# FFN weight scales from sums of squares taken ahead, a new order of the down phase, and weight work inside the units alone

## The chip, the cores and the metric

The kernel runs on one core of one Trainium2 chip. Its time is device time in microseconds: 2755.78 us is the median of three runs of the kernel before (2755.2 to 2758.46). The core has a matrix engine (PE; its weight loads are listed apart as PEld), three engines for elementwise work (DVE, ACT, POOL), and a queue engine (SP) that issues most DMAs. Each engine takes its instructions in the order in which the program gives them; they wait for each other through semaphores.

## The reference, cut to what matters

One transformer block in float32: a sequence S of 2048 rows, width D = 576, 32 heads of 18, and a gated FFN of width 4608.

```python
def _A_ref(x, wqkv, wo):
    qkv = (x @ wqkv).reshape(B, S, 3, H, Dh).transpose(2, 0, 3, 1, 4)
    q, k, v = qkv[0], qkv[1], qkv[2]
    p = _softmax(jnp.einsum("bhqd,bhkd->bhqk", q, k) * Dh ** -0.5, axis=-1)
    return jnp.einsum("bhqk,bhkd->bhqd", p, v).transpose(0, 2, 1, 3).reshape(B, S, D) @ wo

def _B_ref(x, w_gate, w_up, w_down):
    g = jnp.einsum("bsd,df->bsf", x, w_gate)
    u = jnp.einsum("bsd,df->bsf", x, w_up)
    return jnp.einsum("bsf,fd->bsd", _gelu(g) * u, w_down)

h = x + _A_ref(_layernorm(x, axis=-1), A_wqkv, A_wo)
h2 = h + _B_ref(_layernorm(h, axis=-1), B_w_gate, B_w_up, B_w_down)
```

`w_gate` and `w_up` are 576 x 4608, `w_down` is 4608 x 576. The change lies in the last line (`_B_ref`), and in a piece of the attention phase in which weights for it are read ahead.

## The kernel before, in words

Float32 operands are split into two float16 parts, high and low, after multiplication by a power of two; a product is high·high + high·low + low·high, accumulated in PSUM. The power of two comes from an exponent of the weight block. `exponents` finds it: DVE takes the largest magnitude of each partition (L129), PE turns the 128 maxima into a row (L138, a transpose), DVE takes the maximum of that (L142) and shifts out its exponent. `pow2` makes the scale (`p_s_m`, `p_s_dn`).

After attention comes the FFN. The hidden width is cut into 18 chunks of 256 columns, and a loop over `sc` takes two chunks, c and c+1, at a time. The rows are in two halves, p = 0 and p = 1. One pass of the loop, called a round below, runs for the chunks c and c+1 on p = 1 and the next two on p = 0:

```text
unit(c,1)  unit(c+1,1)  down7(1)  unit(c+2,0)  unit(c+3,0)  down7(0)
```

`unit` forms gate and up with Strassen's seven products (Winograd's form): 14 products of 7 matmuls each (L1175), alternately for gate (banks g) and up (banks u), called product 0 to 13 here. ACT copies banks out, since a bank is accumulated on later: product 10 adds to the gate bank that product 8 wrote, so it waits for ACT's copy of it (L1226); product 11 waits for L1230. GELU (L1180) is on ACT, sums and the gating (L1183) on DVE, the hidden value's high part (L1191) on ACT and its low part (L1194) on POOL. The last two products leave a tail on DVE (L1258, L1183, L1266, L1267). After `yield` number k a step of other work can be taken from an iterator `side`; `beside` does that.

`down7` does the down projection of two chunks with seven products as well (HA11 ... HS4), each for two row tiles k. It accumulates in three pairs of banks, X, B and Z (L1286), and DVE adds the bank to the output rows in `nat` (L1291; L1296 adds one bank to both halves). The eight row tiles then leave to DRAM (`nat_d`, L1301) and the other half's tiles are fetched (L1320).

The side work is the weights of the chunks to come. A matrix (gate or up) of a chunk is loaded by eight DMAs on SP (`load_matrix`, L977 and L979) into four of the eight parts of the buffer W8. There is one W8, so the next load waits for the last reads of this one. `split_matrix` then takes the exponent, forms four sums on POOL (L993, S1 to S4), and cuts them to float16: ACT writes three high parts (L1013: parts 4 to 6, which need the DMAs alone, then S1 and S2, then S3 and S4) and DVE the low parts (L1027, L1029). After the first low part the load of the next matrix is issued. `split_down7` scales the down weights (L1136), forms sums on POOL (L1138 to L1145) and cuts seven parts (L1132 on ACT, L1133 on DVE).

The order on PE, ACT, DVE, POOL and, after attention, SP is that of the code, written by hand. In the kernel before, a round's side work starts in unit(c,1) with the exponent of the first matrix, cuts that matrix in unit(c+1,1), and runs on through down7(1), unit(c+2,0) and unit(c+3,0). The exponents of the first two chunks are taken in the attention phase: while the first row maxima of the attention are formed, a loop of 30 steps runs 'sums', a chain that ends in `raw_norms`, on raw weights that POOL's DMAs bring to WK (`raw_loads`).

## Time and profile before

| | |
|---|---|
| median of 3 runs | 2755.78 us |
| the profiled execution | 2758.85 us, span 2757.0 us |
| busy in the span | PE 94%, DVE 84%, ACT 63%, POOL 38% |
| attention, with what stands ahead of it | until about 1,400 us |
| FFN rounds | about 151 us each |
| granted TensorE clock, mean | 0.977 |

The span runs from the first to the last instruction; the profiled execution's 2758.85 us has 1.85 us around it, and lies 3.07 us above the median. PE's busy share says little here: a matmul's recorded time contains its passage through the array, so matmuls overlap in the records. What a stage loses is read from the starts of the products, and from the idle time before an instruction, which the timeline gives in square brackets with what ended it.

### The profile page before, as it was taken

To read this page: it belongs to the slowest core of one execution; us is meant where nothing else is said; L and a number is where in the kernel's file an instruction comes from. 1 tells how busy PE (TensorE), PEld (TensorE's weight loads), DVE (VectorE), ACT (ScalarE), POOL (GpSimd) and SP (SyncE) were. 2 spreads that over 40 slices of the span, in tenths; PEclk is the share of its full clock that TensorE was granted. 3 is DMA by queue.
4 is the path that set the end of the run, shared out by engine and by line. 5 is a ranking of instruction groups with operands and counts; after the bars stand their busy time and mean duration, and the time that the engine had idled before them with its cause. 6 is when DMAs were issued, how large, how long until landed. Compare 5 with 4: busy or idle time off the path is not lost.

```text
span 2757.0 us, 54241 instructions
## 1 busy us (share of the span) xinstructions
PE 2594.8 (94%) x20381; PEld 1174.7 (43%) x20381; DVE 2321.2 (84%) x4230; ACT 1740.0 (63%) x3260; POOL 1034.9 (38%) x1274
## 2 busy tenths in 40 slices
PE   8999999999999999999999988898989898988989
PEld 4533333333333333333355545454445454544545
DVE  7479999999999999998676778788787878787885
ACT  6229999999999999997744334343343433343432
POOL 4202532323232323235853344444443334434432
PEclk9999999999999999999999999999999999999999
DMA  8521010101010101011344223222222223232212
GB/s 221 139 90 30 19 44 16 44 16 42 16 45 16 44 17 42 18 30 36 70 99 88 73 80 101 97 70 76 91 90 90 99 88 107 80 111 86 79 62 82
DMA packets 204761, 189.06 MB, mean 69 GB/s; under 512 B 92504, under 2 KB 151404, under 8 KB 204498
## 3 DMA queue, kind: packets, MB, share of 16 engines
q1 hardware_dynamic: 195758, 169.27, 20.6%
q0 software_dynamic: 8608, 16.33, 2.4%
q8 instruction: 159, 2.61, 0.4%
q14 instruction: 104, 0.85, 0.1%
q10 hardware_dynamic: 132, 0.01, 0.0%
HBM read 115.44 MB, written 50.40 MB: 60 GB/s over the span
## 4 chain that ended last, share of the span: by engine, by line
PE 70%; DVE 16%; issue 5%; ACT 3%; DMA 2%; POOL 2%; SPq 1%; DVEq 0%; ACTq 0%; POOLq 0%
PE bank L673 18%; PE more L1175 8%; PE bank L1175 7%; PE quad L615 7%; PE bank L615 6%; PE more L1286 4%; PE bank L1286 4%; PE quad L300 4%; PE quad L665 4%; PE bank L300 4%; PE bank L665 3%; DVE mx L625 3%; PE more L300 1%; DMA A<-in_B_w_up_dram 1%; DVE W L1029 1%
## 5 line engine op out<-in xcount | busy, mean ns | idle before, releaser
L667 ACT ACTIVATE WK<-quad 128x512 f32<-128x512 f32 x1170 | 656.3, 621 | 26.0 <-PE quad L665 23.6
L673 PE MATMUL bank<-WK,V 128*32 128x256 f32 x8192 | 607.7, 389 | 2.6 <-DVE nat L688 0.6
L625 DVE TENSOR_REDUCE mx<-quad 128x1 f32<-128x512 f32 x836 | 554.0, 685 | 9.0 <-PE quad L665 1.5
L667 ACT ACTIVATE WK<-bank 128x512 f32<-128x512 f32 x878 | 504.9, 622 | 12.0 <-PE bank L665 10.2
L625 DVE TENSOR_REDUCE mx<-bank 128x1 f32<-128x512 f32 x716 | 477.3, 685 | 35.5 <-PE bank L615 26.8
L1175 PEld LDWEIGHTS <-W 128*128 128x128 f16 x2394 | 242.6, 101 | 341.4 <-issue 85.5
L673 PEld LDWEIGHTS bank<-WK,V 128*32 128x32 f32 x8192 | 190.4, 109 | 268.5 <-issue 201.9
L698 POOL TENSOR_TENSOR rp<-rc,minus_one 128x4 f32<-128x4 f32 x112 | 111.2, 1012 | 380.1 <-DMA rc<-nat 377.9
L1175 PE MATMUL bank<-X,W 128*128 128x512 f16 x792 | 225.3, 382 | 0.0
L993 POOL TENSOR_TENSOR A<-A 128x384 f32<-128x384 f32 x136 | 142.7, 1065 | 193.3 <-DVE V L1208 99.3
L1175 PE MATMUL bank<-V,W 128*128 128x512 f16 x720 | 212.3, 395 | 0.5 <-ACT WK L1217 0.5
L615 PE MATMUL quad<-W 54*128 54x512 f16 x514 | 191.3, 383 | 0.0
L1286 PEld LDWEIGHTS <-WK 128*128 128x128 f16 x1472 | 147.3, 100 | 97.1 <-issue 54.2
L1286 PE MATMUL more<-nat,WK 128*128 128x288 f16 x736 | 142.4, 294 | 48.6 <-DVE nat L1291 48.6
L615 PEld LDWEIGHTS <-W 54*128 54x128 f16 x1024 | 74.5, 94 | 241.8 <-issue 227.5
L1013 ACT ACTIVATE W<-A,p_s_m 128x768 f16<-128x768 f32 (+1 forms) x78 | 79.0, 1036 | 149.1 <-DVE p_s_m L173 149.1
L665 PE MATMUL quad<-A 56*128 56x512 f16 x584 | 172.4, 381 | 0.3
L615 PE MATMUL quad<-A 54*128 54x512 f16 x462 | 171.8, 383 | 0.1
L615 PEld LDWEIGHTS <-A 54*128 54x128 f16 x1024 | 71.2, 94 | 231.5 <-issue 216.5
L665 PE MATMUL quad<-W 56*128 56x512 f16 x586 | 168.2, 382 | 0.1
L1175 PE MATMUL more<-V,W 128*128 128x512 f16 x414 | 125.3, 439 | 36.0 <-ACT nat L1226 16.9
L615 PE MATMUL bank<-A 54*128 54x512 f16 x442 | 152.3, 383 | 1.9 <-DMA A<-qk_hi 1.8
(460 smaller groups left out, 5136.7 us busy)
## 6 DMA issues: line engine op xcount, KB each, us to landing
nat_d<-nat SPq DMA_DIRECT2D x120, 288.0 KB
nat<-nat_d SPq DMA_DIRECT2D x120, 288.0 KB
A<-in_B_w_down_dram SPq DMA_DIRECT2D x8, 1152.0 KB
nat<-rc SPq DMA_DIRECT2D x32, 256.0 KB
A<-in_B_w_gate_dram SPq DMA_DIRECT2D x64, 128.0 KB
A<-in_B_w_up_dram SPq DMA_DIRECT2D x64, 128.0 KB
qk_hi<-tmp SPq DMA_DIRECT2D x36, 128.0 KB
qk_lo<-tmp SPq DMA_DIRECT2D x36, 128.0 KB
```

The lines of the kernel that those rows point to most:

```text
L300: nc.tensor.matmul(dst, a, b, start=(i == 0), stop=(i == len(pairs) - 1))
L615: nc.tensor.matmul(pm[:, :TB], Q[r, q0 : q0 + P], keys, start=True, stop=True)
L625: nc.vector.tensor_reduce(dst, pm[:, :TB], axis=AX.X, op=ALU.max)
L665: nc.tensor.matmul(pS[:, :TB], K[r, kt * P : (kt + 1) * P], Q[r, qc * TB : (qc + 1) * TB], start=True, stop=True)
L667: nc.scalar.activation(pes[(2 * kt + hh // 2) % NPE][:, hh % 2], pS[:, :TB], AF.Exp, scale=ex_reg)
L673: nc.tensor.matmul(acc[32 * hh : 32 * hh + 32, qs], Vg[n // NB][:, kt * G4 + hh * VC : kt * G4 + hh * VC + 32], pes[(2 * kt + hh // 2) % N ...
L698: nc.gpsimd.tensor_tensor(rc[:, c : c + 4], den[:, c : c + 4], minus_one.to_broadcast([P, 4]), op=ALU.pow)
L993: op(W8[:, d], W8[:, a], W8[:, b])
L1013: by = hi_on or (lambda dst, src, k: nc.scalar.activation(dst, src, AF.Copy, scale=k))
L1029: nc.vector.scalar_tensor_tensor(wh[r, a:b, 2], W8[r, a:b, 2], s[r], wh[r, a:b, 2], op0=ALU.mult, op1=ALU.subtract)
L1175: nc.tensor.matmul(bank, w, x_, start=start and i == 0, stop=i == len(mm) - 1, skip_group_check=not start)
L1286: nc.tensor.matmul(bank[:, :HALF], a, b, start=start and k == 0, stop=k == len(mm) - 1, skip_group_check=not start)
```

## The change

Scales. The maxima give way to sums of squares: ACT squares the weights in place with a running sum per partition (L992, `square`), PE multiplies the sums with a matrix of ones (L972), and DVE takes half the exponent (`frobenius`, four small instructions). So the exponents for a round must be known ahead. For the round after the next they are found by `scan_weights` beside unit(c,1) (four blocks of raw rows of gate and up) and `scan_down` beside unit(c+2,0) (two blocks of w_down). The raw rows lie in the space of `nat` for the time between the leaving of its tiles and the next down phase; SP issues the loads (L984, L988), and the fetch of the output rows (L1039, L1056) stands behind the squares. The first round's exponents come from `next_norms` in the attention phase: ten DMAs on POOL's queue and six squares on ACT.

Weight work. It is taken out of down7 and starts anew in each of two units: matrices gate and up of c+2 in unit(c+1,1), of c+3 in unit(c+2,0), the down weights in unit(c+3,0) from its first step on. `split_known` is `split_matrix` without the exponent.

Down phase. The order of the products is new: HS1 and HA12 are begun with their first chunk alone, HA22 is accumulated last in X, and each product has one add of half a row (seven per tile, L1408).

```diff
+    def frobenius(q, name):
+        n = q.shape[1]
+        pb = next(m_ring)
+        nc.tensor.matmul(pb[:, :n], ones, q, start=True, stop=True)
+        yield
...
+    def square(v, q):
+        nc.scalar.activation(v, v, AF.Square, accum_out=q)
...
+    def scan_weights(sc):
+        v = [view(nat1, 8 * D * i, (2 * D,)) for i in range(4)]
+        jobs = [(w, c) for w in (w_gate, w_up) for c in (2 * sc, 2 * sc + 1)]
+        q = small.tile([P, 4], F32, tag="fq4", name="fq_a")
+        for _ in range(2):
+            yield
+        for i in range(4):
+            chunk_rows(v[i], *jobs[i], nc.sync)
+            if i % 2:
+                yield
+        for _ in range(4):
+            yield
+        for i in range(4):
+            square(v[i], q[:, i : i + 1])
+            yield
+        for t in range(2 * TPB):
+            nc.sync.dma_start(nat[:, t], nat_d[:, 2 * TPB + t])
+        yield from frobenius(q, ("w", sc))
+
+    def scan_down(sc):
...
+        for _ in range(2):
+            yield
+        for i in range(2):
+            down_rows(v[i], 2 * sc + i, nc.sync)
+        for _ in range(5):
+            yield
+        for i in range(2):
+            square(v[i], q[:, i : i + 1])
+            yield
...
+        yield from frobenius(q, ("d", sc))
...
+    def split_known(c, m, then, at=0, sums=True):
...
+        e = exps[("w", c // 2)][:, 2 * m + c % 2 : 2 * m + c % 2 + 1]
+        s = pow2(e, -1, 266, f"s_m{m}")
...
+        if sums:
+            form_sums()
+        high(0)
+        yield
+        for k, (a, b) in enumerate(cuts):
+            high(k + 1)
+            nc.vector.scalar_tensor_tensor(wl[:, a:b], W8[:, a:b, :2], s, wh[:, a:b, :2], ...
...
+            if k == at:
+                then()
+            yield
...
         for i0 in range(0, TPB, 2):
-            for m, bs, start, n in ((HA11, Xs, True, 0), (HA22, Bs, True, 0), (HS1, Zs, True, 1),
-                                    (HS2, Xs, False, 1), (HA12, Bs, True, 0), (HS3, Xs, False, None),
-                                    (HS4, Zs, False, 1)):
+            j0 = TPB + i0
+            for m, bs, start, chunks in ((HA11, Xs, True, both), (HS1, Zs, True, (0,)), (HA12, Bs, True, (0,)),
+                                         (HS1, Zs, False, (1,)), (HS2, Xs, False, both),
+                                         (HA12, Bs, False, (1,)), (HS3, Xs, False, both),
+                                         (HS4, Zs, False, both), (HA22, Xs, False, both)):
...
-    sums = chain(norm_wo(), raw_norms())
+    sums = chain(norm_wo(), raw_norms(), next_norms())
...
-        if i == AHEAD // 4:
+        if i == AHEAD // 12:
             raw_loads()
-        if i >= AHEAD // 3:
-            take(sums)
+        if i >= AHEAD // 6:
+            take(sums, 1 + (i >= 3 * AHEAD // 4))
...
-        beside(unit(c, 1), side, head=0 if sc else 7)
...
+        if sc == 0:
+            run(unit(c, 1))
+        elif not last:
+            beside(unit(c, 1), scan_weights(sc + 1))
...
+        side = chain((form_sums() for _ in range(1)), pause(1),
+                     split_known(c + 2, 0, lambda: load_matrix(w_up, c + 2), sums=False), pause(1),
+                     split_known(c + 2, 1, lambda: load_matrix(w_gate, c + 3)))
+        beside(u, side)
...
+            run(down7(1, dsc, False))
...
+        side = chain(split_known(c + 3, 0, lambda: load_matrix(w_up, c + 3)), pause(1),
+                     split_known(c + 3, 1, lambda: load_down(sc + 1), 2))
+        ahead = scan_down(sc + 1) if sc else iter(())
+        for _ in unit(c + 2, 0):
+            take(side)
+            take(ahead)
...
+        dn = split_down7(sc + 1)
+        beside(unit(c + 3, 0), dn)
...
-        run(down7(0, dscs[-1], sc == NCH // 2 - 2, True))
+        run(down7(0, dscs[-1], sc == NCH // 2 - 2))
```

Three places in the last full round show what moves. The first is ACT in unit(c+1,1), around the copies that products 10 and 11 wait for (L1226 and L1230 before, L1342 and L1346 now). `p_s_m` is the scale; the 128x1152 row is the first high part of the up matrix, which waits for the six DMAs of its raw parts, and the 128x768 rows wait for POOL's sums. Before:

```order
L1217 COPY A<-bank_66 128x512 [waits PE_49,Pool_49]
L1226 COPY V<-more_16161 128x512 [waits PE_49,Pool_49]
L1230 COPY tmp_83<-bank_66 128x512 [waits PE_49]
L1180 ACTIVATE V<-V,p_gsc_23484 128x512 [waits DVE_49]
L1180 ACTIVATE tmp_83<-more_16161,p_gsc_23484 128x512 [waits PE_49]
L1191 CAST W<-V 128x512 [waits DVE_49]
L1013 ACTIVATE W<-A,p_s_m_24357 128x1152 [waits DMAHW3_49,DMAHW2_49,DMAHW6_49,DMAHW1_49,DMAHW7_49,DMAHW0_49,DVE_49]
```

The same place after the change:

```order
L1333 COPY tmp_83<-bank_66 128x512 [waits PE_49,Activation_49]
L1137 ACTIVATE W<-A,p_s_m_25304 128x1152 [waits DMAHW5_49,DMAHW4_49,DMAHW6_49,DMAHW3_49,DMAHW7_49,DMAHW0_49,DVE_49]
L1342 COPY V<-more_16193 128x512 [waits PE_49,Activation_49]
L1137 ACTIVATE W<-A,p_s_m_25304 128x768 [waits Pool_49]
L1346 COPY WK<-bank_66 128x512 [waits PE_49]
L1296 ACTIVATE V<-V,p_gsc_24519 128x512 [waits DVE_49]
L1137 ACTIVATE W<-A,p_s_m_25304 128x768 [waits Pool_49]
```

Both copies stood ahead of the up matrix's first high part; now the first copy stands behind it, and the second behind the sums S1 and S2 as well.

The second place is ACT in unit(c+2,0), from the copy for product 9 to that for product 11. Before:

```order
L1217 COPY nat<-bank_66 128x512 [waits PE_49,Activation_49]
L1013 ACTIVATE W<-A,p_s_m_24748 128x1152 [waits DMAHW5_49,DMAHW4_49,DMAHW6_49,DMAHW3_49,DMAHW7_49,DMAHW2_49,DVE_49]
L1226 COPY A<-more_16161 128x512 [waits PE_49,Activation_49]
L1013 ACTIVATE W<-A,p_s_m_24748 128x768 [waits Pool_49]
L1230 COPY V<-bank_66 128x512 [waits PE_49]
```

After the change, where L992 is a square of raw rows of w_down and `fq_b` its sums:

```order
L1333 COPY tmp_83<-bank_66 128x512 [waits PE_49,Activation_49]
L1137 ACTIVATE W<-A,p_s_m_25691 128x1152 [waits DMAHW5_49,DMAHW4_49,DMAHW6_49,DMAHW3_49,DMAHW7_49,DMAHW0_49,DVE_49]
L1137 ACTIVATE W<-A,p_s_m_25691 128x768 [waits Pool_49] x2
L992 ACTIVATE nat,fq_b<-nat 128x1152 [waits DMAHW3_49]
L1342 COPY tmp_83<-more_16193 128x512 [waits PE_49,Activation_49]
L992 ACTIVATE nat,fq_b<-nat 128x1152 [waits DMAHW4_49,DMAHW2_49,DMAHW1_49]
L1346 COPY V<-bank_66 128x512 [waits PE_49]
```

Here the copy for product 10 moved from behind one high part to behind all three and a square.

The third place is PE in unit(c,1), between products 12 and 13, where nothing but the unit's own matmuls stood before. `fq_a` holds the sums of the four squares, `ones` is the matrix of ones:

```order
L1291 LDWEIGHTS A
L1291 MATMUL more_16195<-X,A 128x512
L972 MATMUL bank_69<-fq_a,ones 128x4 [waits Activation_49]
L1291 LDWEIGHTS W
L1291 MATMUL bank_68<-X,W 128x512 [waits DVE_49]
```

Product 13 now stands behind a matmul that waits for ACT's fourth square. In unit(c+2,0) a matmul on `fq_b` stands in the same way between products 9 and 10.

More of the change, by code (lines that the diff above doesn't have):

```diff
@@ new lines, in scan_down @@
+    def scan_down(sc):
+        v = [view(nat1, 8 * D * i, (2 * D,)) for i in range(2)]
+        q = small.tile([P, 2], F32, tag="fq2", name="fq_b")
+        for _ in range(2):
[6 more added lines that the diff above has]
+            square(v[i], q[:, i : i + 1])
+            yield
+        for t in range(2 * TPB):
+            nc.sync.dma_start(nat[:, t], nat_d[:, t])
+        yield from frobenius(q, ("d", sc))
@@ L1272, in unit, with down7, product @@
         yield
-    def down7(p, dsc, last, more):
+    def down7(p, dsc, last):
         Xs, Bs, Zs = ([banks[k], banks[3 + k]] for k in (1, 0, 2))
-        def product(bank, m, i, start):
+        def product(bank, m, i, start, chunks=(0, 1)):
             tsl = slice(i * P, (i + 1) * P)
             mm = []
-            for c in range(2):
+            for c in chunks:
                 w = slice(c * HALF, (c + 1) * HALF)
@@ L1495, in tile_block, with fetch_rows @@
-        beside(unit(c, 1), side, head=0 if sc else 7)
+        def fetch_rows(t0):
+            for t in range(2 * TPB):
+                nc.sync.dma_start(nat[:, t], nat_d[:, t0 + t])
+        if sc == 0:
+            run(unit(c, 1))
+        elif not last:
+            beside(unit(c, 1), scan_weights(sc + 1))
+        else:
+            beside(unit(c, 1), (fetch_rows(2 * TPB) for _ in range(1)))
+        u = unit(c + 1, 1)
+        if last:
+            run(u)
+            run(down7(1, dsc, True))
+            break
```

142 lines of the change are left out of this document (81 added, 61 removed).

## The prediction

> **What bounds the kernel now.** I read the page first (PE is 94% busy in its record, so little is to be seen there), then one round of the FFN, as a stretch and in PE's timeline, then the other engines where PE waits. This is the round from 1748.36 us (columns: length, then busy time and count of PE, PEld, DVE, ACT, POOL, then granted clock, DMA share, GB/s), with two undisturbed products from the chain of waits and two adds of a down phase:
>
> ```profile
> 1748.36:1899.25 150.89, 134.17 (x734) 73.75 (x734) 122.17 (x204) 58.21 (x89) 62.95 (x50) 0.94 0.27 90
> 1779.08 1.51 PE more L1175 x7
> 1798.83 1.52 PE bank L1175 x7
> 1768.83 0.52 DVE L1291 SCALAR_TENSOR_TENSOR nat<-bank,p_dsc,nat 128x288 f32<-128x288 f32 x1 [0.22 <-PE bank L1286]
> 1769.56 0.52 DVE L1291 SCALAR_TENSOR_TENSOR nat<-more,p_dsc,nat 128x288 f32<-128x288 f32 x1 [0.22 <-PE more L1286]
> ```
>
> A product of a unit takes 1.51 us. The adds wait for PE and come 0.73 apart, so that is the pace of a down product. A round has 56 of each: 56 x 1.51 + 56 x 0.735 = 125.8 us, and it took 150.9. PE loses 25.1 us per round although DVE is 81% and ACT 39% busy: what bounds the FFN is no engine's sum but waits in the written order. Here they are, PE's rows with the idle time ahead of them, and the clock behind three of them:
>
> ```profile
> 1748.36 3.15 PE L1175 MATMUL more<-V,W 128*128 128x512 f16 x7 [3.44 <-ACT tmp L1226]
> 1762.75 0.53 PE L1286 MATMUL more<-nat,WK 128*128 128x288 f16 x3 [2.22 <-DVE nat L1291]
> 1806.91 1.67 PE L1175 MATMUL more<-V,W 128*128 128x512 f16 x7 [0.53 <-ACT V L1198]
> 1831.46 0.88 PE L1286 MATMUL more<-nat,WK 128*128 128x288 f16 x3 [3.07 <-DVE nat L1291]
> 1883.93 0.69 PE L138 MATMUL bank<-id,am_dn 128*128 128x128 f32 x2 [5.18 <-DVE am_dn L133]
> 1899.25 1.01 PE L1175 MATMUL more<-V,W 128*128 128x512 f16 x2 [3.79 <-ACT nat L1226]
> 1748.40:1751.30 2.90, 2.90 (x8) 0.95 (x7) 2.90 (x4) 1.55 (x3) 1.11 (x2) 0.50 0.00 0
> 1762.80:1766.00 3.20, 3.20 (x27) 2.56 (x27) 3.20 (x8) 0.12 (x1) 3.12 (x4) 1.00 0.00 0
> 1831.50:1834.50 3.00, 3.00 (x13) 1.83 (x13) 2.95 (x5) 0.97 (x2) 1.88 (x3) 0.50 0.11 32
> ```
>
> After idle times of 3.44 and 3.07 us the clock is 0.50 for some 3 us, so such a wait costs 1.5 us more; after 2.22 us it stays at 1.00. With that the waits from 1762 on are 2.2 (down7(0), behind DVE's late tail), 0.5, 4.6 (down7(1), where DVE also cuts weights), 6.7 and 0.7 of transposes (the exponent of w_down), and 5.3 (product 10 of unit(c+3,0), behind the down weights on ACT): 20.0 of the 25.1; the rest is small pieces.
>
> **What the change removes.** The w_down exponent, 7.4 us, about 1 us of small waits for the other exponents, and the weight work in down7(1), part of 4.6 us. If nothing new came, up to 13 us per round would be gained.
>
> **What it adds, stage by stage.** The weight work now runs in units, among the copies in ACT's order. These rows give its lengths: groups of the round on ACT and DVE, the accumulator read behind a square, the load of an up matrix and POOL's sums behind it, and unit(c+2,0) before.
>
> ```profile
> L1013 ACT ACTIVATE W<-A,p_s_m 128x768 f16<-128x768 f32 x6 | 5.5, 927 | 0.0
> L1013 ACT ACTIVATE W<-A,p_s_m 128x1152 f16<-128x1152 f32 x3 | 3.8, 1256 | 19.0 <-DVE p_s_m L173 19.0
> L1136 ACT ACTIVATE A<-A,p_s_dn 128x1152 f32<-128x1152 f32 x2 | 2.4, 1249 | 0.0
> L1180 ACT ACTIVATE tmp<-tmp,p_gsc 128x512 f32<-128x512 f32 x4 | 2.9, 722 | 4.7 <-DVE tmp L1204 4.0 <-DVE tmp L1227 0.7
> L1296 DVE SCALAR_TENSOR_TENSOR nat<-bank,p_dsc,nat 128x576 f32<-128x576 f32 x4 | 3.3, 816 | 0.0
> 125.32 0.20 ACT L155 ACTIVATION_READ_ACCUMULATOR A<-nat 128x1 f32 x1
> 1808.05 1.02 DVE L1027 SCALAR_TENSOR_TENSOR A<-A,p_s_m 128x768 f16<-128x768 f32 x1 [2.32 <-ACT A L1013]
> 1809.10 0.61 DVE L1029 SCALAR_TENSOR_TENSOR A<-A,p_s_m 32x384 f16<-32x384 f32 x1
> 1809.13 0.38 SPq L977 DMA_DIRECT2D A<-in_B_w_up_dram  x1
> 1813.60 3.58 DMA A<-in_B_w_up_dram
> 1817.30 4.44 POOL L993 TENSOR_TENSOR A<-A 128x384 f32<-128x384 f32 x4 [1.97 <-DMA A<-in_B_w_up_dram]
> 1850.27 0.38 SPq L977 DMA_DIRECT2D A<-in_B_w_up_dram  x1
> 1863.31 1.26 ACT L1013 ACTIVATE W<-A,p_s_m 128x1152 f16<-128x1152 f32 x1 [1.76 <-DVE p_s_m L173]
> 1865.24 0.58 ACT L1226 COPY A<-more 128x512 f32<-128x512 f32 x1 [0.68 <-PE more L1175]
> ```
>
> An up matrix takes long to come. Its first DMA goes out when the first low part of the gate matrix ends (1809.07), the last is issued from 1813.60 and has landed 3.58 later: 8.2 us from low part to landing. The eight DMAs are issued 0.64 apart, so the sixth, with which ACT's first high part can start, is there after 6.9 (an estimate from these rows). POOL then needs 1.1 per sum. The new code leaves four products, 6 us, between load and use.
>
> *unit(c+2,0)*, time v from its start. ACT's first high part of the gate matrix starts behind the copy for product 0, at 2.2, DVE's low part ends at 4.5, and SP loads the up matrix. Before, that load went out at 1850.27, ahead of the unit: its product 8 had ended by 1865.2, so it began at 1851.4. Now the sixth DMA has landed at 11.4, the high part runs until 12.65; all is there at 12.7, sums end at 13.8, 14.9, 16.0, 17.0, the last high part at 17.9. A square is priced by its nearest row, a 128x1152 scaling of 1.25, and 0.1 for the accumulator read, most of which overlaps: 1.35, so until 19.3. Only then stands the copy for product 10 (until 19.8), due at 13.8. And between products 9 and 10 PE has the matmul on the second square's sum, ready at 21.2. Product 10, due at 15.1, starts at 21.3: 6.2 us, and 1.5 of clock. 7.7 (5 if squares were nearly free; 9).
>
> *unit(c,1)*. Squares stand behind products 8 to 11. ACT from 13.8 on: two copies (0.58), two GELUs (0.72), a cast (0.6) and four squares, 8.6 us, until 22.4. The matmul of ones ahead of product 13 waits for the last; product 12 ends at 19.6. That is 2.8 us, between the idle times that did and did not cost clock, so half of 1.5: 3.5 (1.5 to 4.5). On SP the raw rows stand behind the eight leaving tiles but have 14 us to land, and behind the squares stand the output rows, needed 25 us later: nothing.
>
> *unit(c+1,1)*, time u from the end of the product before. Its start is bound by the tail, which stays:
>
> ```profile
> 1800.38 0.69 DVE L1258 TENSOR_TENSOR V<-bank,V 128x512 f32<-128x512 f32 x1 [0.22 <-PE bank L1175]
> 1804.09 1.64 DVE L1267 TENSOR_TENSOR V<-A,tmp 128x512 f32<-128x512 f32 x1
> 1806.29 0.58 ACT L1198 COPY V<-more 128x512 f32<-128x512 f32 x1
> ```
>
> The first copy ends 6.7 us after that product (1800.2), so 0.5 is lost as before. The weights start two steps later than they did: scale at 7.6, high part until 8.9, GELU, gating until 10.6, low part until 11.7. The sixth DMA has landed at 18.5, high part until 19.8, copy until 20.3: product 10, due at 15.7, starts 4.7 late. The copy for product 11 stands behind S2 as well (landed 19.9, S2 22.1, high part 23.0, copy 23.5): 1.7 more, in which the slow clock is hidden. 6.4 (3.9 with no lag on DVE at all; 7.5).
>
> *down7(1)*. DVE waited too. From 20.3 it has a sum and the first low part (until 22.7), from 23.5 a sum and a gating, two low parts of 1.4, five instructions of 0.75, a gating of 1.4 and two of 1.64 of the tail: until 36.6. PE has product 13 done at 28.6, then 30 down matmuls (3.7 us) that need nothing, with 0.2 for HS1's low part, and then wants bank X back, whose add ends at 37.1: 4.6 and 1.5 of clock, 6.1 (2.2, as at 1762.75; 8). In the old order 36 matmuls stood there, 0.7 us more cover. The adds are 7 x 0.52 per tile for 6 x 0.52 and one of 0.82, under PE's 5.15 either way. HA22 and the next HA11 share a bank with one product between: 0.1.
>
> *unit(c+3,0)*. Eleven small instructions on DVE follow the tail (2 us), then ACT's two scalings (2.5) ahead of the copy for product 5. Its casts wait for POOL's sums, and DVE's low parts stand ahead of the gate's sum:
>
> ```profile
> L1145 POOL TENSOR_TENSOR A<-A 128x576 f32<-128x576 f32 x2 | 3.6, 1794 | 0.2
> L1133 DVE TENSOR_TENSOR nat<-A,nat 128x576 f16<-128x576 f32 x8 | 11.7, 1509 | 3.8 <-ACT nat L1132 3.8
> ```
>
> In ACT's order: scalings until 9.9, copy for product 5 at 10.4 (due 8.2); three casts, POOL's second sum at 13.1, a cast, GELU behind DVE at 15.5, two casts, copy for product 8 at 17.2 (due 14.9); a cast behind the gating (18.9), one of HA22, copy for product 9 at 20.6 (due 18.7). 2.2 + 2.3 + 1.9 = 6.4 (3 to 8), where 5.3 was lost.
>
> *down7(0)*: 2.2 as before and 0.7 for the new order, 2.9.
>
> Sum: 7.7 + 3.5 + 0.5 + 6.4 + 6.2 + 6.4 + 2.9 = 33.6, and 1 of small pieces: 34.6 against 25.1, 9.5 more. Seven rounds are full: 67. The first has no squares and loses its w_down exponent too; by the same terms 5 more. The last has no weight work: 0.
>
> *Attention.* PE is the bound where the squares go, and ACT has room:
>
> ```profile
> 160.00:180.00 20.00, 20.00 (x98) 8.13 (x97) 15.91 (x31) 4.67 (x8) 1.46 (x5) 1.00 0.31 98
> WK<-in_B_w_gate_dram POOLq DMA_DIRECT2D x4, 288.0 KB, 9.2
> ```
>
> Six squares are 8 us on an engine 23% busy; raw rows land 9 us after their issue on POOL's queue, about three steps of the loop, so ACT may wait, and PE's evacuations with it: 2 (0 to 8). In all 67 + 5 + 2 = 74. The profiled execution's 2758.85 becomes 2833; it lies 3 above the median, so **2830**.
>
> **The skill.** The Trainium skill (DMA: Bandwidth & Descriptors, Anatomy of one DMA) gives one DMA a fixed cost of about 2.0 us, where the row has 3.58 for a small one; by the page's figure the up matrices would land an estimated 1.5 us earlier in two units and the sum would be 7 x 3 = 21 less, 2809. The row decides.
>
> **Rivals.** *The up matrix is in time* (faster): if it lands before it stands in the way, unit(c+1,1) loses 0.5 in all, unit(c+2,0) 2 for its squares, down7(1) 3: 15 less per round, 19.6 against 25.1, so 7 x 5.5 = 39 less, 2719 with the attention's 2. For it: in unit(c+2,0) the first high part stands ahead of the copy already (1863.31, 1865.24), and PE loses nothing. Against: there it was loaded ahead of the unit. It decides where all has landed 7 us into unit(c+2,0); the rows say 12.7. 0.17. *The new waits just replace the old* (same): with stages near their lower ends, 25 per round. 0.06. *Waits feed on each other*: each longer wait brings half clock and a later DVE, 42 per round: 7 x 17 and 10, about 2885. 0.15. My forecast has 0.62, with 2790 to 2860 as its own range.
>
> So slower 0.77, faster 0.17, same 0.06 (within 0.2%, 5.5 us, about what a measurement of this kernel can tell from no change). The range 2712 to 2888 leaves out gains beyond the first rival's and the far end of the last, less than 0.2.
>
> **What would show it.** Right: PE idle 5 us or more ahead of product 10 of unit(c+2,0), released by ACT, with its copy L1342 right behind a square L992; POOL's sums waiting for the up matrix in both units; rounds of about 160 us without L138. Wrong: ACT's first high part of an up matrix ahead of the end of product 8, or rounds under 148 us.

## The result, and the profile after

| | before | after |
|---|---|---|
| median of 4 runs each | 2757.12 us (2755.2 to 2767.48) | 2871.73 us (2866.34 to 2878.34) |
| ratio, 95% interval | | 1.0409 (1.0372 to 1.0446) |
| profiled execution, span | 2758.85, 2757.0 us | 2866.34, 2864.5 us |
| granted clock, mean | 0.977 | 0.966 |

Slower, as forecast, and inside the stated range; but 115 us slower where 74 was forecast, and outside the 2790 to 2860 that the prediction gave its own forecast. First the six stages of one round of the changed kernel, in order from unit(c,1) to down7(0) (columns as in the prediction: length, busy time and count of PE, PEld, DVE, ACT, POOL, granted clock, DMA share, GB/s):

```profile
1973.53:1996.54 23.01, 21.55 (x102) 9.70 (x100) 8.20 (x11) 12.62 (x22) 2.69 (x3) 1.00 0.87 221
1996.54:2027.05 30.51, 23.92 (x99) 10.17 (x98) 23.37 (x35) 13.62 (x21) 17.98 (x15) 0.89 0.18 56
2027.05:2052.50 25.45, 21.10 (x169) 16.34 (x168) 20.95 (x35) 3.61 (x6) 10.82 (x9) 1.00 0.20 70
2052.50:2082.69 30.19, 23.35 (x103) 10.33 (x100) 18.24 (x35) 15.15 (x22) 7.35 (x6) 0.89 0.49 168
2082.69:2114.62 31.93, 25.16 (x99) 10.39 (x98) 23.54 (x32) 16.24 (x27) 16.59 (x12) 0.89 0.19 64
2114.62:2137.59 22.97, 20.78 (x169) 16.41 (x168) 18.31 (x31) 3.02 (x6) 6.96 (x5) 1.00 0.17 63
```

Undisturbed, a unit takes 14 x 1.51 = 21.1 us and a down phase 28 x 0.735 = 20.6. Three of the four units lose 9 to 11 us, each with a mean clock of 0.89. These are the waits (PE's rows of the timeline from the end of one round to the end of the next; in brackets the idle time and who ended it):

```profile
1956.59 0.53 PE L1402 MATMUL more<-nat,WK 128*128 128x288 f16 x3 [2.19 <-DVE nat L1408]
1994.79 0.39 PE L972 MATMUL bank<-fq_a,ones 128*128 128x4 f32 x2 [1.46 <-ACT nat L992]
2018.40 3.15 PE L1291 MATMUL more<-V,W 128*128 128x512 f16 x7 [6.59 <-ACT V L1342]
2035.56 0.53 PE L1402 MATMUL more<-nat,WK 128*128 128x288 f16 x3 [3.39 <-DVE nat L1408]
2074.62 0.59 PE L972 MATMUL more<-fq_b,ones 128*128 128x2 f32 x2 [6.84 <-ACT nat L992]
2094.90 2.73 PE L1291 MATMUL bank<-V,W 128*128 128x512 f16 x7 [3.80 <-ACT A L1317]
2105.38 2.96 PE L1291 MATMUL bank<-V,W 128*128 128x512 f16 x7 [2.28 <-ACT tmp L1333]
```

The transposes of the w_down exponent (L138, 5.18 us in a round before) are gone. In their place stand a wait for ACT's copy ahead of product 10 of unit(c+1,1), one for the matmul of ones ahead of product 10 of unit(c+2,0), and two in unit(c+3,0).

The lengths of the stages, taken from the starts of the products in the traces, are used for all that follows: means of the seven full rounds, in us; "start" is when the first product of the FFN begins. The last column is the median time.

| kernel | start | unit (c,1) | unit (c+1,1) | down7(1) | unit (c+2,0) | unit (c+3,0) | down7(0) | round | time |
|---|---|---|---|---|---|---|---|---|---|
| undisturbed | | 21.1 | 21.1 | 20.6 | 21.1 | 21.1 | 20.6 | 125.7 | |
| before | 1399.6 | 21.3 | 23.2 | 28.1 | 21.3 | 34.7 | 22.9 | 151.4 | 2757.1 |
| after | 1409.1 | 23.0 | 31.2 | 24.9 | 30.2 | 31.9 | 23.0 | 164.2 | 2871.7 |
| 1 no up load | 1408.5 | 23.0 | 28.0 | 26.2 | 28.0 | 31.7 | 23.0 | 160.0 | 2828.6 |
| 2 no scan | 1407.5 | 21.2 | 29.6 | 27.6 | 27.9 | 31.0 | 23.0 | 160.2 | 2837.8 |
| 3 late up | 1404.0 | 23.0 | 21.2 | 33.8 | 29.7 | 32.5 | 23.0 | 163.3 | 2848.6 |
| 4 old order | 1403.7 | 23.0 | 30.1 | 27.0 | 30.6 | 32.0 | 22.2 | 164.9 | 2862.7 |
| 5 no raw rows | 1399.4 | 23.0 | 31.5 | 25.7 | 30.3 | 31.9 | 23.0 | 165.4 | 2867.7 |
| 6 no load, early scale | 1406.4 | 23.0 | 24.3 | 28.9 | 28.5 | 31.2 | 23.0 | 159.0 | 2819.0 |
| 7 early everything | 1408.1 | 22.7 | 26.5 | 27.1 | 22.9 | 32.4 | 23.0 | 154.6 | 2786.4 |
| 8 the same, old order | 1407.1 | 22.7 | 26.8 | 26.8 | 22.9 | 32.6 | 22.2 | 153.9 | 2783.3 |
| 9 three suspects off | 1407.1 | 21.2 | 24.1 | 28.7 | 24.8 | 31.0 | 23.0 | 152.7 | 2782.9 |
| 10 no down cut | 1408.6 | 23.0 | 30.6 | 27.5 | 30.6 | 21.8 | 23.0 | 156.5 | 2803.1 |
| 11 down exponent alone | 1397.8 | 21.3 | 23.1 | 28.1 | 23.0 | 35.8 | 22.2 | 153.5 | 2771.5 |
| 12 the same, reordered | 1404.9 | 21.3 | 21.5 | 28.2 | 22.9 | 24.1 | 34.6 | 152.6 | 2767.9 |

The 107.5 us between the two profiled executions are 7 x 12.8 in the rounds, 9.5 ahead of the FFN, 6.2 in the first round and 2.4 in the last, where the new down order takes 24.9 us for 22.5 (0.2 is rounding). The medians are 7 us further apart, since the profiled execution of after is the fastest of its four and that of before lies 1.7 above its median; what the slower ones of after lose is in no trace here.

### The profile page after: what moved, and what is told of

Its sections match the earlier page's. It is cut to its first block, busy times and chain, and to the rows that moved or that the text cites. A ratio compares the mean times of both kernels' runs of the same rounds, so it can differ in the third digit from the quotient of the medians.

```text
span 2864.5 us, 54158 instructions
## 1 busy us (share of the span) xinstructions
PE 2621.2 (92%) x20365; PEld 1175.0 (41%) x20365; DVE 2251.1 (79%) x4031; ACT 1788.2 (62%) x3356; POOL 1039.2 (36%) x1284
## 4 chain that ended last, share of the span: by engine, by line
PE 65%; DVE 16%; ACT 6%; DMA 4%; issue 4%; SPq 2%; POOL 2%; DVEq 0%; ACTq 0%; POOLq 0%
PE bank L673 17%; PE quad L615 6%; PE more L1291 6%; PE bank L1291 6%; PE bank L615 5%; PE more L1402 5%; PE bank L1402 5%; PE quad L665 4%; PE bank L300 3%; PE quad L300 3%; DVE mx L625 3%; PE bank L665 3%; DVE nat L1249 2%; ACT nat L992 2%; DMA A<-in_B_w_up_dram 1%
## 5 line engine op out<-in xcount | busy, mean ns | idle before, releaser
L1291 PE MATMUL bank<-V,W 128*128 128x512 f16 x720 | 230.5, 425 | 50.8 <-ACT A L1317 15.2
L1310 POOL TENSOR_TENSOR WK<-tmp,WK 128x512 f16<-128x512 f32 x53 | 70.2, 1325 | 277.4 <-ACT WK L1307 277.4
L615 PEld LDWEIGHTS <-A 54*128 54x128 f16 x1024 | 71.4, 94 | 234.9 <-issue 220.0
```

Source lines behind the costliest of these rows:

```text
L615: nc.tensor.matmul(pm[:, :TB], Q[r, q0 : q0 + P], keys, start=True, stop=True)
L1291: nc.tensor.matmul(bank, w, x_, start=start and i == 0, stop=i == len(mm) - 1, skip_group_check=not start)
L1310: nc.gpsimd.tensor_sub(at(hl, k), v, at(hh, k))
```

## Experiments

**Four single suspects.** The first asks how much of the loss is the up matrix that lands too late.

```diff
-                     split_known(c + 2, 0, lambda: load_matrix(w_up, c + 2), sums=False), pause(1),
+                     split_known(c + 2, 0, lambda: None, sums=False), pause(1),
```

(and the same for c+3).

> The changed kernel without the loads of the up matrices in units (c+1,1) and (c+2,0): POOL, ACT and DVE cut what lies in the buffer, so all engine work stays and only the wait for the transfer goes. Theory (ACT's in-order copies stand behind an up matrix that lands too late): PE's loss in unit(c+1,1) falls from 9.4 us a round to about 2, in unit(c+2,0) from 8.5 to about 2.5 (the squares stay), in down7(1) by about 1; 14 to 15 a round, some 105 in all, about 2765. Rival (the squares and the matmul of ones in unit(c+2,0)): that unit keeps 6 or more, 2810 or above. Rival (DVE's scales are late beside POOL): both units keep most of their loss, 2850.

2828.64 us, 1.0246 (1.0226 to 1.0265) of before: 43 less than after, not 105. unit(c+1,1) lost 3.2 us and unit(c+2,0) 2.2, and down7(1) took 1.3 back. My theory named the wait that ended last, but not the only one. The rows of this kernel's timeline show who stood behind it, in unit(c+1,1) and then in unit(c+2,0):

```profile
1998.37 1.12 DVE L1147 SCALAR_TENSOR_TENSOR A<-A,p_s_m 32x256 f16<-32x256 f32 x1
...
2000.21 0.15 DVE L173 TENSOR_SCALAR p_s_m<-pi_s_m 128x1 int32<-128x1 int32 x1
...
2000.40 1.25 ACT L1137 ACTIVATE W<-A,p_s_m 128x1152 f16<-128x1152 f32 x1 [5.68 <-DVE p_s_m L173]
...
2002.17 3.00 PE L1291 MATMUL more<-V,W 128*128 128x512 f16 x7 [4.96 <-ACT V L1342]
...
2054.42 0.59 PE L972 MATMUL more<-fq_b,ones 128*128 128x2 f32 x2 [4.25 <-ACT nat L992]
```

With no transfer to wait for, ACT's first high part waits 5.68 us for the up matrix's scale. That is two tiny DVE instructions which the code emits behind all six low parts of the gate matrix; the copy for product 10 (L1342) still stands behind that high part. In unit(c+2,0) the wait for the squares' matmul is what is left.

The second takes the scans out: `scan_weights` and `scan_down` only fetch the output rows, and the exponents of round 1 serve later rounds.

```diff
-        for i in range(4):
-            square(v[i], q[:, i : i + 1])
-            yield
...
-        yield from frobenius(q, ("w", sc))
+        exps[("w", sc)] = exps[("w", 1)]
```

> The changed kernel without the scans of rounds 1 to 6: no raw rows loaded, no squares, no matmul of ones; every later round uses the exponents of round 1. Theory of the late up matrix: only the squares' own share goes, about 1.1 a round in unit(c,1) and 2.5 to 3.5 in unit(c+2,0), 6 rounds, 22 to 28 in all, about 2845. Rival (the squares are the cause of the wait ahead of product 10): unit(c+2,0) falls from 8.5 to under 2 and unit(c,1) to 0.5, 8 a round, 2823 or less.

2837.76 us, 1.0286 (1.0267 to 1.0304): 34 less than after, between theory and rival. (The scans stand in seven rounds, not six as written there and in later expectations.) unit(c,1) is back at 21.2, and unit(c+2,0) loses 2.3: that much goes when the squares and their loads are taken away alone, so they are not the main cause there. But down7(1) takes back 2.7.

The third leaves nothing out; the up matrix is cut three products later, so that the copies for products 10 and 11 come first.

```diff
-                     split_known(c + 2, 0, ..., sums=False), pause(1),
+                     split_known(c + 2, 0, ..., sums=False), pause(4),
-        side = chain(split_known(c + 3, 0, lambda: load_matrix(w_up, c + 3)), pause(1),
+        side = chain(split_known(c + 3, 0, lambda: load_matrix(w_up, c + 3)), pause(4),
```

> The changed kernel with the up matrix cut three products later in both units (pause 4 instead of 1), nothing left out: the copies for products 10 and 11 stand ahead of ACT's first high part. Theory of the late up matrix: the loss in unit(c+1,1) falls from 9.4 to 1 to 3 a round and in unit(c+2,0) from 8.5 to 3 to 4; the low parts that now fall into the tail add 0 to 3 to down7(1), and the down weights load two products later, 0 to 2 in unit(c+3,0); net 6 to 12 a round, 2780 to 2825. Rival (the wait is only moved: the tail's copies and casts stand behind the same landing): 2860 to 2880.

2848.63 us, 1.0332 (1.0314 to 1.0351): 23 less, between the two. unit(c+1,1) is perfect, 21.2 us for 31.2, and down7(1) is 33.8 for 24.9; in unit(c+2,0) the high part stands between the two squares now, and the matmul of ones waits as before. Rows around and behind the start of its down7(1), at 2332.2 us:

```profile
2331.42 1.26 ACT L1137 ACTIVATE W<-A,p_s_m 128x1152 f16<-128x1152 f32 x1 [0.87 <-DMA A<-in_B_w_up_dram]
...
2332.64 5.34 POOL L1124 TENSOR_TENSOR A<-A 128x384 f32<-128x384 f32 x4 [8.46 <-DMA A<-in_B_w_up_dram]
...
2339.59 0.42 PE L1402 MATMUL more<-nat,W 128*128 128x288 f16 x1 [6.63 <-POOL W L1310]
...
2347.98 0.53 PE L1402 MATMUL more<-nat,WK 128*128 128x288 f16 x3 [3.88 <-DVE nat L1408]
```

ACT now waits only 0.87 us for the transfer, but POOL's sums still wait for it, 8.46. PE waits for what stands behind them: POOL's low parts of the hidden values, which come after the up matrix's sums, and DVE's adds, which come after its low parts. In unit(c+1,1) and down7(1) the rival was right about the mechanism: the wait was only moved, behind the same landing. The time was below its range.

The fourth puts the old order of the down products back into the changed kernel (the old `down7`, whole).

> The changed kernel with the old order of the down phases (one add of both halves, HA22 second, banks as before), the rest as changed. Theory: the order is worth about 1 us a down phase, so 7 x 1 to 2 less, 2855 to 2872. Rival (the new order is a main cause, with its seven adds per tile and less cover in front of the first bank taken back): down7(1) falls from 4.8 and down7(0) from 2.4 by 4 together, 2842 or less.

2862.7 us, 1.0374 (1.0356 to 1.0393). The interval overlaps that of after, and no effect of the order is shown: down7(0) gains 0.8 a round and the last down phase 2.4, down7(1) loses 2.1 behind a unit(c+1,1) that is 1.1 shorter. A round is 0.7 longer. The profiled executions of the two are only 1.4 us apart, and in that the attention, which the edit does not touch, was 5.4 shorter.

**The attention phase.**

```diff
-        for i in range(5):
-            fetch(i)
...
-            if i == 0:
-                fetch(5)
```

> The changed kernel without the six loads of raw rows that go ahead of the squares in attention; the squares run on what the first six loads left. Theory (the transfers delay attention, not ACT's squares): the first unit starts at 1399 to 1402 us of the span as before the change, where it stood at 1403 to 1409 in the five kernels with them; 2 to 9 us less, 2862 to 2870. Rival (the squares themselves in ACT's order): the first unit stays at 1403 to 1409, 2872.

The FFN starts at 1399.4, as the theory has it. But that start moves by itself: it is 1404.9 in the twelfth kernel, which has no raw rows either, and 1403.7 in the fourth, which has them. The time, 2867.71 us, 1.0414 (1.0394 to 1.0433), does not tell it from 2871.7, since its rounds are 1.2 longer, for which I have no cause. So the stretch itself, measured from the first to the eleventh instruction of L619 (ACT's Relu in the row maxima); they are the first and the last of the seven in each L619 row here. First before, then after, then this kernel, each with its window from 160 to 220 us, and one wait of after:

```profile
L619 ACT ACTIVATE nat<-bank x7: 592/598/667, 164.3 to 235.7; 128x512 f32<-128x512 f32 x7
160.00:220.00 60.00, 58.20 (x334) 21.87 (x337) 46.81 (x88) 23.78 (x44) 1.46 (x5) 0.97 0.29 88
```

```profile
L619 ACT ACTIVATE nat<-bank x7: 592/597/666, 164.8 to 244.0; 128x512 f32<-128x512 f32 x7
160.00:220.00 60.00, 55.49 (x251) 20.34 (x249) 38.62 (x79) 23.14 (x41) 8.07 (x14) 0.90 0.51 137
185.15 0.60 ACT L352 ACTIVATE tmp<-quad 128x512 f16<-128x512 f32 x1 [6.89 <-DMA qk_hi<-tmp]
```

```profile
L619 ACT ACTIVATE nat<-bank x7: 592/597/666, 164.3 to 236.0; 128x512 f32<-128x512 f32 x7
160.00:220.00 60.00, 58.13 (x330) 21.78 (x333) 45.17 (x90) 30.22 (x55) 0.73 (x4) 0.97 0.26 78
```

71.4 us before, 79.2 after, 71.7 with the squares but without the transfers. In the ten kernels with the raw rows it is 75.1 to 79.3, in the four without 71.4 to 72.9. So the squares cost next to nothing there (0.3 us, with ACT 30.22 us busy instead of 23.78) and the transfers 4 to 8: they raise the DMA share of this window from 0.29 to 0.51, and the small stores of q and k (`qk_hi`) that ACT's buffers wait for land late.

**Several waits side by side?** Two kernels take suspects away together: the sixth has no up loads and makes the up scale with the gate scale, ahead of the low parts; the ninth has, besides, no scans.

```diff
+        if m == 0:
+            made[c] = scale(c, 1)
```

> No loads of up matrices, as in the first of these experiments, and also the up matrix's scale made together with the gate matrix's, ahead of DVE's low parts. Theory now (two waits lie beside each other ahead of product 10: the landing, and the up matrix's scale, which stands in DVE's order behind six low parts that POOL slows): unit(c+1,1) falls from 28.0 us to 22 to 24, unit(c+2,0) from 27.9 by 0 to 3, and the time to 2775 to 2805. Rival (POOL's sums of the up matrix are the second wait): unit(c+1,1) stays above 26, 2820.

> Three suspects off together: no loads of up matrices, the up matrix's scale made ahead of the low parts, and no scans in rounds 1 to 6 (later rounds use round 1's exponents). Theory (each unit has several waits beside each other, so that one taken away alone shows the next): unit(c+1,1) 21.2 to 23 us and unit(c+2,0) 21.2 to 23, where one alone left 24.2 to 29.6 and 27.8 to 28.6; down7(1) stays at 27 to 30 behind DVE's tail, unit(c+3,0) at 30 to 32; a round 146 to 151, the time 2735 to 2775. Rival (the parts simply add): a round 155, 2790 to 2800.

Sixth: 2819.01 us, 1.023 (1.0213 to 1.0247). unit(c+1,1) falls to 24.3, so landing and scale together are 6.9 of its 10.1. unit(c+2,0) does not follow, and down7(1) takes back 2.7 more: the time misses what the theory asked for. Ninth: 2782.87 us, 1.0088 (1.007 to 1.0107). A round takes 152.7, where the sixth's 5.2 and the second's 4.0 off would give 155.0: the waits overlap, but less than I had said. With the transfers, the late scale and all squares gone the rounds are still 1.3 longer than before the change.

**Better lead times, all work kept.** The seventh takes the squares two steps earlier, POOL's sums a unit earlier, cuts the gate from step 0 on, loads the up matrix behind it, cuts it seven products later, and makes every scale at once; the eighth has the old down order.

> Nothing left out; the weight work stays in units, but each step starts as soon as its data allow: squares two steps earlier, POOL's sums of the gate matrices a unit earlier, gate matrices cut from the first step, up matrices loaded one to two products earlier and cut seven products later instead of four, all scales made ahead of the low parts and of the tail. Theory (lead times between load, scale and use are what the change got wrong, not the work itself): a round falls from 163.9 to 145 to 153 us, the time to 2735 to 2790. Rival (DVE and POOL side by side have too much work for these units, at the lengths they have beside each other): a round stays above 157, 2820 or more.

> The kernel of the experiment before with the old order of the down phases. Theory: with no weight work in the down phases the old order loses 22.2 us each where the new one loses 23.0, so 14 x 0.8 less and 2.4 in the last one: 10 to 14 us under the experiment before. Rival (the old order needs its banks earlier behind a late DVE, 2.6 a round in down7(1) as in the fourth experiment): 5 to 20 us above it.

2786.37 us, 1.0114 (1.0087 to 1.0142), and 2783.25, 1.0104 (1.0087 to 1.0121): 85 us of the 115 lost are back. unit(c+2,0) is at 22.9, from 30.2, with no work left out, though some of it now stands in its neighbours; there the change's trouble was lead time in the main. The seventh's time lies inside the theory's range, but a round, 154.6, lies between theory and rival. The old order was to bring 10 to 14 us; the medians differ by 3, with intervals that overlap. The scale ready early, unit(c+3,0) still takes 32.4, with another wait (rows from 8.5 us into it):

```profile
2048.43 1.64 DVE L1395 TENSOR_TENSOR tmp<-tmp,V 128x512 f32<-128x512 f32 x1
...
2050.62 0.58 ACT L1326 COPY nat<-more 128x512 f32<-128x512 f32 x1
...
2051.25 3.15 PE L1303 MATMUL more<-V,W 128*128 128x512 f16 x7 [3.94 <-ACT nat L1326]
```

The copy of product 0, for which product 4 waits, stands behind the casts of the unit before, which wait for DVE's tail; the eleven small instructions of the scale now stand ahead of that tail.

**The down weights.** The tenth leaves out their cutting in unit(c+3,0) (a `return` behind the scale), the eleventh has only their exponent taken ahead, on the kernel before.

> The changed kernel without the cutting of the down weights in unit(c+3,0) of rounds 1 to 6: no scalings, sums, casts and low parts there; the scale itself is still made and the weights still loaded. Theory (those copies in ACT's order and low parts in DVE's order are what PE waits for in that unit): unit(c+3,0) falls from 31.9 to 21.5 to 23 us, 6 rounds, 53 to 62 less, 2810 to 2820. Rival (the unit starts behind the late tail of the one before it): it stays at 26 or more, 2840 or more.

2803.07 us, 1.0158 (1.0139 to 1.0177); unit(c+3,0) takes 21.8 for 31.9. The down cut is 10.1 of its 10.8 us of loss, as the theory says. The time is below its 2810 to 2820, which counted six rounds for seven, although down7(1) takes back 2.6 a round.

```diff
-        ed = yield from exponents([view(A, W8O + 4 * 2 * D * i, (1, 2 * D)) for i in range(2)], "dn")
+        ed = exps[("d", sc)] if sc > 1 else (yield from exponents(
+            [view(A, W8O + 4 * 2 * D * i, (1, 2 * D)) for i in range(2)], "dn"))
...
-        beside(unit(c + 2, 0), side)
+        ahead = scan_down(sc + 1) if sc else iter(())
+        for _ in unit(c + 2, 0):
+            take(ahead)
+            take(side)
```

> One part of the change alone, on the kernel before: only w_down's exponent from sums of squares taken ahead in unit(c+2,0), rounds 1 to 6; the gate and up matrices keep their maxima, their places and the old order of the down phases. Theory (the part removed was worth its 7.4 us, and the squares cost little where the up matrix is loaded ahead of the unit): unit(c+3,0) falls from 34.8 to 27 to 29, unit(c+2,0) rises from 21.3 by 0 to 1.5; 5 to 7 a round, 2714 to 2728. Rival (the squares and their matmul of ones give it back in unit(c+2,0), as they seem to in the changed kernel): that unit rises by 4 or more, 2740 to 2765.

2771.49 us, 1.0049 (1.0032 to 1.0066): 0.5% slower than before, against both theory and rival. The transposes are gone, the squares cost 1.7 in unit(c+2,0), and unit(c+3,0) takes 35.8 for 34.7:

```profile
2194.96 0.17 DVE L173 TENSOR_SCALAR p_s_dn<-pi_s_dn 128x2 int32<-128x2 int32 x1
...
2195.21 2.40 ACT L1179 ACTIVATE A<-A,p_s_dn 128x1152 f32<-128x1152 f32 x2 [2.89 <-DVE p_s_dn L173]
2197.52 0.56 ACT L1241 COPY tmp<-more 128x512 f32<-128x512 f32 x1
...
2198.13 3.15 PE L1218 MATMUL more<-V,W 128*128 128x512 f16 x7 [9.21 <-ACT tmp L1241]
```

Without the steps of the exponent ahead of them, the scalings were emitted before the unit's first copy, and waited for a scale that DVE makes behind its tail. One wait of 9.21 us replaced 5.18 and 3.79. The twelfth reorders just that: a unit's last three casts behind the next unit's first copies, the scale at product 4, the scalings behind product 7, one or two casts a step from product 9 on, HA22 last.

> The kernel of the experiment before, in a new order of emission alone: the last three casts of a unit (A12, HS3, HS4 and POOL's low parts of them) stand behind the first two copies of the next unit; the down weights' scale is made at product 4 of unit(c+3,0), the scalings stand behind product 7's instructions and the casts one by one behind products 9 to 13; down7(0) has the new order, in which HA22 comes last. Theory (the exponent's 7.4 us could not be won because the scalings moved ahead of that unit's first copy, 9.2 us of idle time in PE): unit(c+3,0) falls from 35.8 to 25 to 30, down7(0) rises by 0.8 to 4, a round takes 143 to 150 and the time is 2700 to 2748, under the kernel before. Rival (DVE's 28 us of work in that unit is the limit, whatever ACT's order): unit(c+3,0) and down7(0) together fall by less than 3 from 58.0, 2752 to 2772.

2767.86 us, 1.0039 (1.0025 to 1.0052). unit(c+3,0) takes 24.1 instead of 35.8, and down7(0) 34.6 instead of 22.2: 58.7 together for 58.0, as the rival said. Its windows of the two stages, and PE's waits in the second:

```profile
2188.78:2212.89 24.11, 21.47 (x100) 9.56 (x99) 19.70 (x32) 13.84 (x22) 12.37 (x10) 1.00 0.15 50
2212.89:2246.70 33.81, 24.32 (x170) 17.41 (x169) 25.62 (x40) 5.86 (x10) 14.38 (x12) 0.85 0.19 64
...
2215.89 0.30 PE L1395 MATMUL more<-nat,W 128*128 128x288 f16 x1 [2.23 <-POOL W L1247]
...
2220.82 0.88 PE L1395 MATMUL bank<-nat,WK 128*128 128x288 f16 x3 [3.13 <-DVE WK L1311]
```

DVE is busy 45.3 us in this pair, where PE undisturbed needs 41.7; in after's unit(c+1,1) and down7(1) it is busy 44.3. With this work on DVE, at these lengths, no order of ACT's lets PE run through such a pair: 3.6 us are lost at least. But the pair takes 57.9, and in 12.6 of them DVE is not busy. So the rival's reason accounts for the smaller part of the loss, and a better order is not excluded. No version here beats the kernel before.

## Why the prediction was right in sign and short in size

Losses per round against the undisturbed stages, in us:

| step | forecast | measured | what was off |
|---|---|---|---|
| unit(c,1), squares | 3.5 | 1.9 | wait 1.46 for 2.8, as ACT's stretch from its first copy to the last square took 7.4, not 8.6; no slow clock |
| unit(c+1,1), with the tail's 0.5 | 6.9 | 10.1 | low parts beside POOL; slow clock |
| down7(1) | 6.2 | 4.3 | wait 3.39 for 4.6 in the round shown, and no slow clock behind it; shorter where unit(c+1,1) is longer (1, 2 and 6 show the exchange) |
| unit(c+2,0) | 7.7 | 9.1 | idle 6.84 for 6.2; slow clock as forecast |
| unit(c+3,0) | 6.4 | 10.8 | idle 6.8, at other products than forecast; slow clock left out |
| down7(0) | 2.9 | 2.4 | |
| small pieces | 1.0 | | |
| sum | 34.6 | 38.5 | |

Three stages came 9.0 us longer than forecast, the others and the small pieces 5.0 shorter, so the sum is nearer than its terms: part of that is luck. (56 products of each kind at the paces given are 125.7 us, where the prediction writes 125.8.) "9.5 more per round" was 12.8; "first round 5" was 6.2, "last 0" was 2.4, "attention 2 (0 to 8)" was 9.5 in this execution, outside its bounds.

*The clock* is the rule that the prediction had wrong. It took the cost from the length of a wait: 1.5 us behind 3.07, nothing behind 2.22. In after, the wait of 3.39 in down7(1) cost no clock, and that of 2.28 in unit(c+3,0) was followed by half clock. What decides is at the end of this document.

*unit(c+2,0)* came as written. The rows:

```profile
2065.99 4.83 POOL L1124 TENSOR_TENSOR A<-A 128x384 f32<-128x384 f32 x4 [2.73 <-DMA A<-in_B_w_up_dram]
...
2070.86 0.94 ACT L1137 ACTIVATE W<-A,p_s_m 128x768 f16<-128x768 f32 x1 [0.97 <-POOL A L1124]
2071.70 1.15 ACT L992 ACTIVATE nat<-nat 128x1152 f32<-128x1152 f32 x1
...
2072.84 0.56 ACT L1342 COPY tmp<-more 128x512 f32<-128x512 f32 x1
2073.31 1.16 ACT L992 ACTIVATE nat<-nat 128x1152 f32<-128x1152 f32 x1
```

These rows, with PE's wait of 6.84, are the first sign that the prediction named. The last high part ends 19.3 us into the unit (forecast 17.9), the copy right behind a square at 20.9 (19.8), the matmul of ones at 22.1 (21.2). PE's own record puts the wait down to the second square, and the first and second experiments show that the transfer and the squares hold 2.2 and 2.3 of it each when taken away alone: the chain was right, but a term in it is not what its removal brings.

*unit(c+1,1)*, as far as the scale, came on time:

```profile
2001.27 1.08 DVE L978 TENSOR_SCALAR fe<-fe 128x4 int32<-128x4 int32 x1
...
2004.15 0.15 DVE L173 TENSOR_SCALAR p_s_m<-pi_s_m 128x1 int32<-128x1 int32 x1
...
2006.90 1.75 DVE L1145 SCALAR_TENSOR_TENSOR A<-A,p_s_m 128x768 f16<-128x768 f32 x1
2008.69 1.40 DVE L1147 SCALAR_TENSOR_TENSOR A<-A,p_s_m 32x384 f16<-32x384 f32 x1
...
2016.62 1.25 ACT L1137 ACTIVATE W<-A,p_s_m 128x1152 f16<-128x1152 f32 x1 [7.30 <-DMA A<-in_B_w_up_dram]
...
2003.39 4.45 POOL L1124 TENSOR_TENSOR A<-A 128x384 f32<-128x384 f32 x4
...
2017.87 5.00 POOL L1124 TENSOR_TENSOR A<-A 128x384 f32<-128x384 f32 x4 [8.20 <-DMA A<-in_B_w_up_dram]
```

Scale at 7.8 us (7.6). Then the first low part, priced 1.02 and 0.61 from a row in which POOL was idle, took 1.75 and 1.40 beside POOL's sums, which this same change put there; they ended 1.8 later than forecast, and the high part behind the landing started 1.6 later. POOL's sums waited for the up matrix in both units (8.20 here, 2.73 above), as the second sign says. The 2.0 us per DMA that the prediction cites are stated for DMAs issued by POOL, and these are issued by SP: the last load of this up matrix landed 3.71 us after its issue, and the 2809 would have been further off. The 1.7 added for product 11 did not come, since it lies inside the slow clock of product 10, which came on top.

*unit(c+3,0)*: the idle times 0.54, 3.80, 0.15 and 2.28 stand ahead of products 4, 5, 8 and 9 and sum to 6.8. Forecast were 2.2, 2.3 and 1.9 ahead of 5, 8 and 9, 6.4; that the sums agree is luck. The term that failed is the clock, left out behind all of these waits. It was 0.50 for 3.41 us behind the 3.80 and again behind the 2.28, which is 3.4 of the 4.0 us lost beyond the idle times; it also made product 8 due later, so that little of its wait was left. The 3.80 was longer than its 2.2 for the same reason as above, two of the eleven small instructions at 1.1 us instead of 0.16:

```profile
2088.16 1.11 DVE L1215 CUSTOM_DVE_ANT_0 E<-fe 128x4 uint16<-128x4 uint16 x1
2089.31 1.08 DVE L1216 CUSTOM_DVE_ANT_0 fe<-fe,E 128x4 uint16<-128x4 uint16 x1
...
2091.98 2.40 ACT L1252 ACTIVATE A<-A,p_s_dn 128x1152 f32<-128x1152 f32 x2 [2.60 <-issue]
2094.29 0.56 ACT L1317 COPY A<-bank 128x512 f32<-128x512 f32 x1
```

*Attention*: priced as squares on ACT, which cost next to nothing, with 2 for late rows; the cost was the transfers' own, with stores that others wait for landing late, 7.8 of the 9.5 in this execution.

*What the change removes*, "up to 13 us per round would be gained", was read from PE's waits. In the two orders that the eleventh and twelfth experiments tried, the 7.4 of the w_down exponent did not come: DVE's late tail and its work stood right behind. The forecast survived that because it priced unit(c+3,0) anew.

*The rivals.* "The up matrix is in time" was wrong in its condition, since the high part waits 7.30 us for the landing. It would not have been faster either: with no up load at all, the kernel is 43 us faster than after and still 71 slower than before. "Waits feed on each other" had part of what came, low parts that end later and half clock behind the waits of unit(c+3,0); the 38.5 us lost per round lie halfway between the 34.6 forecast and its 42.

## What to carry to other kernels

A wait has a row, but what stands right behind it has none: before pricing a removal, list what each waiting instruction would wait for next, and price a step with the lengths that its instructions have beside the engines that the change sets next to them. Compare each stage's busy time on the second engine with the undisturbed time of the first; where DVE's 45 us stand against PE's 42, no order hides all of DVE's work, and here a new order moved the rest of the wait to the next stage. Work put on an idle engine is cheap, the transfers that feed it need not be.

## What the runs showed of the hardware

DVE beside POOL: instructions of DVE that read two operands in SBUF took longer while POOL's tensor operations ran: a 128x512 sum 1.64 us for 0.68, the 128x768 low part 1.75 for 1.02, the 32-partition low part 1.40 for 0.61. So did small integer instructions on two or four numbers per partition: L1216 1.08 us, where the same on an idle POOL took 0.16 (twelfth kernel), and L978 1.08 on four numbers, where on two with POOL idle it took 0.17. Those on one number per partition kept their length (L173: 0.15 with POOL and without), and so did adds that read a PSUM bank (0.52). The Trainium skill (GPSIMD Engine Reference, Specifications) says that POOL's SBUF interfaces are shared with DVE and contended by instructions with two SBUF inputs or in a two-port mode. The two-input sums agree; that four numbers per partition cost 0.9 us more is this trace's.

The clock: the length of a wait alone does not decide. In after, matmuls kept their pace behind waits of 2.19 us (1956.59) and of 3.39 (2035.56), and ran at half behind 2.28 (2105.38). The trace says why. In all 14 traces of this case the granted clock changes only at times that lie whole multiples of 3.413 us apart (to within 3 ns). These are the stretches between such times around the waits of 3.39 and 2.28 (the second number is PE's busy time):

```profile
2030.51:2033.92 3.41, 1.66 (x14) 1.13 (x13) 3.41 (x3) 1.18 (x3) 3.41 (x3) 1.00 0.01 2
2033.92:2037.34 3.42, 1.78 (x15) 1.43 (x15) 3.40 (x7) 0.87 (x2) 3.42 (x4) 1.00 0.00 0
2102.19:2105.61 3.42, 1.14 (x7) 0.40 (x5) 3.32 (x5) 1.95 (x4) 0.52 (x1) 1.00 0.00 0
2105.61:2109.02 3.41, 3.41 (x10) 1.21 (x9) 0.74 (x3) 0.85 (x3) 1.16 (x1) 0.50 0.36 106
```

The 3.39 us are cut in two, and PE idles 1.75 us in one stretch and 1.64 in the next; the 2.28 lie in one, and the clock is 0.50 through the stretch that follows. Counted over the 14 traces from 1410 us on: behind a stretch at full clock in which PE idled less than 1.8 us the next one was at full clock (4,678 of 4,678), behind more than 2.2 us at half (322 of 322), and in between it was half in 60 of 123. So the same wait costs 1.7 us of clock or nothing, by where it falls. The waits of 2.22 us that the prediction took as too short (before, 1762.75) and of 2.20 in the tenth kernel (2099.03) were cut as well. In the twelfth kernel matmuls keep pace behind the 2.23 at 2215.89, which is cut at 2214.08; one round later a wait of 2.22 lies in one stretch, and the clock falls as it ends, at 2367.68. The Trainium skill (TensorE: Matmul & The Clock Gate, Part 1) has a window of 3.4 us that runs freely; the 3.413 us between changes agree. That the clock falls after a whole idle window does not fit, since 2.28 us of idle time in one were enough.
